# One list scheduler for a whole kernel: decayed attention and two MLPs in fp32, with quads in alternating order and five sums a quad in layer 2

## The chip, the cores and the metric

The kernel runs on one core of a Trainium2 chip. It uses the core's five instruction queues: TensorE (PE, matrix products), ScalarE (ACT), VectorE (DVE), GpSimd (POOL) and SyncE (SP, which issues the DMAs). The metric is the device time of one execution in microseconds (us). Before the change it is 615.07 us, the median of 3 runs (614.79 to 617.62).

## The reference

Three stages follow each other, all in fp32:

```python
# 1. linear attention with decay lam[h], B=2, H=8 heads, S=768, D=64, blocks of 64
intra = einsum(einsum(qb, kb) * Dmask, vb)            # Dmask[i,j] = lam**(i-j) for i >= j
out[:, :, sl] = intra + einsum(qb * lam_pow, kv_state)
kv_state = lam_block * kv_state + einsum(kb_dec, vb)
x = out.transpose(0, 2, 1, 3).reshape(1536, 512)
# 2. MLP 1: 512 -> 2048 -> 512
h = x @ w_in;  x = (h * tanh(softplus(h))) @ w_out     # Mish
# 3. MLP 2: 512 -> 2048 -> 512
h = maximum(x @ w_in, 0);  x = (h * h) @ w_out
```

## The kernel before

Every fp32 product is made of three matmuls of rounded halves: a tensor is split in a high half (a cast, on ACT) and a low half (the tensor less its high half, a subtraction), and `mm3` (L67 to L71) adds high x high, high x low and low x high in one bank of PSUM. Lines L69, L70 and L71 in the profile are these three matmuls. The 1536 tokens are four blocks t of 384.

*Weights* arrive as 64-bit patterns, in slices of 128 hidden columns (input slice io=0, output slice io=1). For each slice SP loads `raw` (L94), ACT makes `absw` (L107), DVE rebuilds the fp32 number with three integer operations (L118, L120, L122), and the result is split: cast on ACT (L138 or L199) and low half on POOL (L146 or L200).

*Attention* is 16 pairs (block t, two heads), the class `Pair`: scores, masks on DVE (L368), state updates on DVE (L363), outputs, and the split of the result into `xh` and `xl` (L398).

*Layer 1* takes the first eight hidden slices plainly, in 32 steps of one block and one slice: h (four times mm3), Mish on ACT, `gh` on ACT (L441), `gl` on POOL (L447), and four y products that accumulate in banks y0 to y3; a finished y goes to SBUF by a copy or a sum on DVE (L473). The other eight slices are taken as pairs j=0 to 3 (256 hidden columns) by two token pairs tp (blocks 2tp and 2tp+1): eight *quads*. A quad computes a 2 x 2 block product with seven products instead of eight (p1, p6, p2, p7, p4, p5, p3), which needs seven factors of the weights (sums of quarters on DVE, L234 to L240) and seven of the tokens (`first_factors`, sums at L513), and sums of the products on DVE (L657, `add`; the output tile is named u). The four results c11, c21, c22, c12 go through Mish, are split (L721, L722) and multiplied with an output slice; these y products of a quad are interleaved with the seven products of the next one as `chunks`.

*Layer 2* has 16 slices, all in 16 quads (`SecondQuad`), with relu and square (L784, L790, L791). There each of the seven products has its own turn in a ring of two banks named h, and seven DVE sums join them. Its token factors are made from layer 1's y (`right_factors`, sums at L591, splits at L579 and L583).

*What sets the order.* Attention and the first 16 steps are a table of operations with durations and due times (`plan`, L832), issued by a list scheduler (`issue`, L908): at each turn, of the operations that can start first, the one with the earliest due time. From step 16 on the order is that of the code. After each chunk of y one `job()` (L149) moves the conversion of weights on by a piece; pieces of factors lie in the list `todo`, and a few are taken behind each product; `wait_for` (L251) converts what a product asks for and isn't there yet. In layer 1 the quads run (0,0), (0,1), (1,0), (1,1), (2,0), (3,0), (2,1), (3,1) as (j, tp), every one in the same inner order, and the y banks are emptied at the end of each half of a quad's blocks.

Of the kernel before, what the change touches and what calls it, by code (L numbers as in the profile page):

```python
# [14 lines left out]
RING, RAW = 8, 5  # L15
PLAIN = 8
FIRST = (0, 4), (4, 8)
SECOND = 4
# [3 lines left out]
SLACK = 0.25  # L22
PLAN = False

# [3 lines left out]
def shares(i, n):  # L28


    if n - 1 <= i <= n + 1:
        return ((1,) * 7, (1, 1, 1, 1, 1, 0, 0), (0,) * 7)[i - n + 1], (4, 3, 3)[i - n + 1]
    return (2,) * 7, 3
# [3 lines left out]
def tile_attn_mlp_mlp(ctx, tc, qkv_in, lam, w1i, w1o, w2i, w2o, out):  # L37
    nc = tc.nc
    pe, act, dve, pool, sp = nc.tensor, nc.scalar, nc.vector, nc.gpsimd, nc.sync

# [9 lines left out]
    CPB = S // P  # L50
    blocks = [(b, c) for b in range(BATCH) for c in range(0, CPB, NC)]

    const = ctx.enter_context(tc.tile_pool(name="const", bufs=1))
    wts = ctx.enter_context(tc.tile_pool(name="wts", bufs=1))
    xp = ctx.enter_context(tc.tile_pool(name="xp", bufs=1))
    gp = ctx.enter_context(tc.tile_pool(name="gp", bufs=2))
    stg = ctx.enter_context(tc.tile_pool(name="stg", bufs=RAW))
    ac = ctx.enter_context(tc.tile_pool(name="ac", bufs=1))
    ar = ctx.enter_context(tc.tile_pool(name="ar", bufs=4))
    ps1 = ctx.enter_context(tc.tile_pool(name="ps1", bufs=1, space=PSUM))  # L60
    ps2 = ctx.enter_context(tc.tile_pool(name="ps2", bufs=2, space=PSUM))
# [997 lines left out]
```

## Time and profile before

| What | Value |
|---|---|
| median of 3 runs | 615.07 us |
| profiled execution, its own time | 619.45 us |
| its span, first to last instruction | 617.7 us |
| mean granted clock of TensorE | 0.973 |
| PE busy | 584.5 us, 95% of the span |
| DVE busy | 420.6 us, 68% |
| POOL busy | 323.9 us, 52% |
| ACT busy | 312.9 us, 51% |

The profile shows one execution. A busy share is a mean over stages with different limits, so it is read together with the table of windows, which gives busy time and the number of matmuls for each stretch of time. The granted clock is the share of full speed that PE was given: 1.00 is 2.4 GHz, and lower values in a window mean that for a part of it PE ran at the lower of its two levels. In the list of waits an entry says which engine waited, at which line, and for which other engine's instruction.

### The profile page before, as it was taken

What the parts mean: (1) busy time and instruction counts of PE and PEld (TensorE: products, weight loads), DVE (VectorE), ACT (ScalarE), POOL (GpSimd) and SP (SyncE); (2) the same over time, 40 slices, a digit from 0 to 9 for tenths busy, and PEclk for the clock granted to TensorE, in tenths of its full rate; (3) what the DMA queues carried; (4) which work ended last, traced back from release to release, by engine and by line L of the source; (5) the groups of instructions that cost most, each with busy time, mean ns of one, the idle gap of its engine ahead of it and who ended that gap; (6) DMA issues with size and microseconds to landing.
All of it is one profiled execution on the core that took longest, in us unless ns stands there. A gap on an engine that the chain in (4) does not pass through costs nothing. (4 is left out here: it accounts for less than half of the span.)

```text
span 617.7 us, 9413 instructions
## 1 busy us (share of the span) xinstructions
PE 584.5 (95%) x3448; PEld 534.7 (87%) x3448; DVE 420.6 (68%) x701; ACT 312.9 (51%) x662; POOL 323.9 (52%) x315
## 2 busy tenths in 40 slices
PE   7799999999887899999999997899999999999997
PEld 6578888999776899999999986788889989888885
DVE  5896677623998778478799693486885678464333
ACT  3464453634442544253545554667654676464441
POOL 3465343426874876272837673467562864273221
PEclk8899999999897989999999997899999999999999
DMA  8867462210420022040400120132230413000112
GB/s 313 298 211 239 119 187 71 69 35 0 137 68 1 0 70 103 0 137 1 136 1 1 34 70 34 35 102 81 91 102 1 133 38 103 1 1 0 52 52 102
DMA packets 15743, 49.89 MB, mean 81 GB/s; under 512 B 1873, under 2 KB 1873, under 8 KB 15697
## 3 DMA queue, kind: packets, MB, share of 16 engines
q1 hardware_dynamic: 15696, 49.29, 24.0%
q8 instruction: 27, 0.44, 0.3%
q14 instruction: 20, 0.16, 0.1%
HBM read 46.14 MB, written 3.15 MB: 80 GB/s over the span
## 5 line engine op out<-in xcount | busy, mean ns | idle before, releaser
L657 DVE TENSOR_TENSOR u<-h,u 128x384 f32<-128x384 f32 x120 | 65.0, 553 | 101.4 <-PE h L71 101.0
L200 POOL TENSOR_TENSOR w<-raw,w 128x256 fp32r<-128x256 f32 (+1 forms) x80 | 78.5, 997 | 17.6 <-ACT w L199 15.0
L69 PE MATMUL h<-xh,w 128*128 128x384 f32 x244 | 84.4, 346 | 0.6 <-ACT w L138 0.6
L70 PE MATMUL h<-xl,w 128*128 128x384 f32 x244 | 83.3, 341 | 1.4 <-DVE xl L398 1.4
L71 PE MATMUL h<-xh,w 128*128 128x384 f32 x244 | 83.2, 341 | 1.0 <-POOL w L146 1.0
L784 ACT ACTIVATE u<-u 128x384 f32<-128x384 f32 x64 | 33.6, 525 | 91.8 <-DVE u L657 91.4
L69 PE MATMUL y<-gh,w 128*128 128x384 f32 x192 | 68.4, 356 | 6.0 <-DVE y L473 4.3
L70 PE MATMUL y<-gl,w 128*128 128x384 f32 x192 | 66.4, 346 | 5.6 <-POOL gl L447 5.6
L447 POOL TENSOR_TENSOR gl<-u,gh 128x384 fp32r<-128x384 f32 x32 | 36.2, 1132 | 66.5 <-ACT gh L441 66.4
L71 PE MATMUL y<-gh,w 128*128 128x384 f32 x192 | 65.8, 343 | 0.1
L120 DVE SCALAR_TENSOR_TENSOR raw<-absw,raw 128x512 uint32<-128x512 uint32 x64 | 60.9, 952 | 4.6 <-ACT absw L107 1.3
L122 DVE SCALAR_TENSOR_TENSOR raw<-raw 128x512 uint32<-128x512 uint32 x64 | 56.6, 884 | 1.5
L657 DVE TENSOR_TENSOR y<-y,y 128x384 f32<-128x384 f32 (+1 forms) x88 | 49.1, 584 | 12.4 <-PE y L71 12.2
L792 POOL TENSOR_TENSOR gl<-u,gh 128x384 fp32r<-128x384 f32 x32 | 35.2, 1100 | 34.7 <-ACT u L791 19.6
L69 PEld LDWEIGHTS h<-xh,w 128*128 128x128 f32 x244 | 46.9, 192 | 5.0 <-issue 1.2
L70 PEld LDWEIGHTS h<-xl,w 128*128 128x128 f32 x244 | 46.8, 192 | 4.4 <-DVE xl L398 1.9
L71 PEld LDWEIGHTS h<-xh,w 128*128 128x128 f32 x244 | 46.5, 191 | 1.6 <-POOL w L146 1.6
L69 PEld LDWEIGHTS y<-gh,w 128*128 128x128 f32 x192 | 36.7, 191 | 10.9 <-DVE y L473 4.3
L107 ACT ACTIVATE absw<-raw 128x512 f32<-128x512 f32 x64 | 43.0, 673 | 6.0 <-DMA raw<-in_w1i_dram 3.2
L118 DVE TENSOR_SCALAR raw<-raw 128x512 uint32<-128x512 uint32 x64 | 44.7, 699 | 0.2
L199 ACT CAST w<-raw 128x256 fp32r<-128x256 f32 (+1 forms) x80 | 36.6, 493 | 15.8 <-DVE raw L122 11.5
L70 PEld LDWEIGHTS y<-gl,w 128*128 128x128 f32 x192 | 37.0, 193 | 7.5 <-POOL gl L447 7.5
(251 smaller groups left out, 1538.9 us busy)
## 6 DMA issues: line engine op xcount, KB each, us to landing
raw<-in_w1i_dram SPq DMA_DIRECT2D x16, 512.0 KB, 4.2
raw<-in_w1o_dram SPq DMA_DIRECT2D x16, 512.0 KB, 3.8
raw<-in_w2i_dram SPq DMA_DIRECT2D x16, 512.0 KB, 3.3
raw<-in_w2o_dram SPq DMA_DIRECT2D x16, 512.0 KB, 4.3
kq<-in_qkv_dram SPq DMA_DIRECT2D x16, 384.0 KB, 4.1
kv<-in_qkv_dram SPq DMA_DIRECT2D x16, 384.0 KB, 4.3
out_dram<-y SPq DMA_DIRECT2D x12, 256.0 KB, 2.0
lam_t<-in_lam_dram SPq DMA_DIRECT2D x1, 4.0 KB, 3.0
```

The source lines that it names most:

```text
L69: pe.matmul(o, lhsT=wh, rhs=xh, start=start, stop=False, **kw)
L70: pe.matmul(o, lhsT=wh, rhs=xl, start=False, stop=False, **kw)
L71: pe.matmul(o, lhsT=wl, rhs=xh, start=False, stop=stop, **kw)
L107: act.activation(a.bitcast(F32), raw[u].bitcast(F32)[:, :, 1], AF.Copy, scale=2.0 ** -112)
L118: dve.tensor_scalar(lo, lo, 29, None, op0=ALU.logical_shift_right)
L120: dve.scalar_tensor_tensor(lo, a, 3, lo, ALU.logical_shift_left, ALU.bitwise_or)
L122: dve.scalar_tensor_tensor(lo, hi, 0x80000000, lo, ALU.bitwise_and, ALU.bitwise_or)
L199: act.copy(hl[0], t)
L200: pool.tensor_tensor(hl[1], t, hl[0].bitcast(F32), ALU.subtract)
L447: pool.tensor_tensor(gl, g, gh.bitcast(F32), ALU.subtract)
L657: dve.tensor_tensor(o, x, y, ALU.add)
L792: pool.tensor_tensor(gl, u, gh.bitcast(F32), ALU.subtract)
```

## The change

`plan`, `job`, `todo`, `wait_for` and the ring allocators are gone. Every instruction of the program is now an operation `op(engine, duration, emit, reads, writes, due)`; what it must wait for follows from the names of the places that it reads and writes. One list scheduler issues all of them. Four more things change with it:

- A subtraction that makes a low half (from step 16 on) and a sum of factors may run on POOL or on DVE; the scheduler takes the engine where it can start first by its own clock. PE's operations get their due time from a running sum of durations (`slot`), and the others get theirs backwards from PE's, less a margin.
- In layer 1 the quads run (0,0), (1,0), (1,1), (0,1), (2,1), (3,1), (3,0), (2,0), and every second one takes its products in another order, with its blocks the other way round. A y bank goes on accumulating from one quad to the next where both work on the same block, and is emptied only when the block changes. In layer 2 the token pairs alternate by groups, with the same effect.
- In layer 2, p2 accumulates on the bank of p1, p4 on that of p7 and p3 on that of p5 (as layer 1 did before), so five DVE sums do instead of seven.
- SP's order of loads is the scheduler's too.

The matmuls are the same in number.

```diff
+    def op(eng, dur, emit, r=(), w=(), due=1e9, after=(), name=""):
...
+        for s in r:
+            need |= writer.get(s, set())
+        for s in w:
+            need |= writer.get(s, set()) | readers.get(s, set())
...
+    def issue():
+        for o in reversed(ops):
+            for n in o.need:
+                least = min(o.eng.values())
+                n.due = min(n.due, o.due - least - LAT - (LAND if "SP" in n.eng else 0) - (0 if "PE" in n.eng else o.early))
...
+                pick = min((x for x in c if x[0] <= r0 + SLACK), key=lambda x: (x[1].due, max(x[0], f)))
+                r = max(f, pick[0])
+                if best is None or r < best[0]:
+                    best = r, e, pick[1]
...
+    def slot(dur):
+        clock[0] += dur
+        return clock[0]
...
+    SUB384 = {"POOL": 1.1, "DVE": 0.6}
+    SUB256 = {"POOL": 0.8, "DVE": 0.5}
+    SUB512 = {"POOL": 1.4, "DVE": 0.8}
...
+    def out_slice(f):
+        if ("o", f) not in done:
+            t, R = bits(PLAIN + f, 1, [V[NI - 1]])
+            done["o", f] = split(whole_w(1, f % 5), t, R, SUB512, 0.66, name=f"o{f}")
+        return done["o", f]
...
+    SUM = {"DVE": 0.8, "POOL": 1.1}
...
+            self.order = ("p1", "p6", "p7", "p5", "p3", "p2", "p4") if turned else ("p1", "p6", "p2", "p7", "p4", "p5", "p3")
+            self.cs = ("c22", "c12", "c11", "c21") if turned else ("c11", "c21", "c22", "c12")
+            if layer:
+                z = "h0", "h1"
+                k = n % 2
+                self.bank = dict(A=z[k], B=z[1 - k], C=z[1 - k], D=z[k])
+            else:
+                self.bank = dict(A="h0", B="h1", C="X", D="Y")
...
+            op(SUB384, 0, lambda e: e.tensor_tensor(v(l), o, v(h.bitcast(F32)), ALU.subtract), O + H_, L_, name=f"gl.{self.n}")
...
+        def p4(self):
+            self.product("C", 2, "T4", True)
+            c = self.q if self.turned else self.temp("c21")
+            self.add(c, self.C, self.q)
+            self.leave("c21", c, c)
...
-        def p2(self):
-            o = self.product(bank("h")[:, :N], 1, "B21")
-            self.relu("c11", self.add(self.p, o, self.p))
...
-        def p5(self):
-            o = self.product(bank("h")[:, :N], 3, "T1")
-            self.add(self.r, o, self.r)
-            self.add(self.q, o, self.q)
-            self.relu("c22", self.r)
...
+        first = [(0, 0), (1, 0), (1, 1), (0, 1), (2, 1), (3, 1), (3, 0), (2, 0)]
...
+        for i, q in enumerate(seq):
             ys = {12: (1, 1, 1, 3, 1, 3, 2) if i else (2, 2, 2, 2, 2, 2, 0), 16: (2, 2, 2, 3, 2, 3, 2)}[len(chunks)]
-            jobs, pops = shares(i, len(order))
-            for name, y, n in zip(qd.NAMES, ys, jobs):
-                getattr(qd, name)()
-                for _ in range(n):
-                    job()
+            for name, y in zip(q.order, ys):
+                getattr(q, name)()
                 for _ in range(y):
                     chunks.pop(0)()
...
```

The change moves instructions on every queue. Three places follow, as rows of an engine's order (row number, line, operation, output and inputs, shape), before and after.

SP's queue from its first load on. Before, lam is loaded first (row 0 of both is a branch):

```order
1 L835 DMA lam_t<-in_lam_dram 128x8
2 L288 DMA kq<-in_qkv_dram 128x768
3 L293 DMA kv<-in_qkv_dram 128x768
4 L288 DMA kq<-in_qkv_dram 128x768
5 L293 DMA kv<-in_qkv_dram 128x768
6 L288 DMA kq<-in_qkv_dram 128x768
7 L94 DMA raw<-in_w1i_dram 128x1024
```

The same place of SP's queue after the change:

```order
1 L379 DMA kq_110<-in_qkv_dram 128x768
2 L381 DMA kv_114<-in_qkv_dram 128x768
3 L379 DMA kq_111<-in_qkv_dram 128x768
4 L297 DMA lam_t<-in_lam_dram 128x8
5 L381 DMA kv_115<-in_qkv_dram 128x768
6 L379 DMA kq_112<-in_qkv_dram 128x768
7 L227 DMA raw_91<-in_w1i_dram 128x1024
```

The load of lam moved from the first place to the fourth, behind two loads of kq and one of kv.

DVE's queue before, where the last pair of attention is over and the first factors and the cuts of the first weight pair begin (L118 to L122 conversion, L234 to L240 cuts of a weight pair, L513 sums of factors; their inputs z, xh, xl are factors in the making):

```order
150 L118 TENSOR_SCALAR raw<-raw 128x512
151 L120 SCALAR_TENSOR_TENSOR raw<-absw,raw 128x512
152 L122 SCALAR_TENSOR_TENSOR raw<-raw 128x512
153 L234 TENSOR_TENSOR absw<-raw 128x256
154 L513 TENSOR_TENSOR z<-xh_428,xl_429 128x384
155 L236 TENSOR_TENSOR absw<-absw,raw 128x256
156 L513 TENSOR_TENSOR z<-z 128x384
157 L238 TENSOR_TENSOR raw<-raw 128x256
158 L513 TENSOR_TENSOR z<-z 128x384
159 L240 TENSOR_TENSOR raw<-raw,absw 128x256
160 L513 TENSOR_TENSOR z<-z 128x384
161 L118 TENSOR_SCALAR raw<-raw 128x512
```

The same place after (L232 to L236 conversion, L272 cuts of a weight pair, L244 a low half of a weight):

```order
154 L232 TENSOR_SCALAR raw_93<-raw_93 128x512
155 L234 SCALAR_TENSOR_TENSOR raw_93<-absw_97,raw_93 128x512
156 L236 SCALAR_TENSOR_TENSOR raw_93<-raw_93 128x512
157 L272 TENSOR_TENSOR absw_96<-raw_93 128x256
158 L272 TENSOR_TENSOR absw_96<-absw_96,raw_92 128x256
159 L232 TENSOR_SCALAR raw_94<-raw_94 128x512
160 L234 SCALAR_TENSOR_TENSOR raw_94<-absw_97,raw_94 128x512
161 L272 TENSOR_TENSOR raw_92<-raw_92,absw_96 128x256
162 L244 TENSOR_TENSOR w_2_65<-absw_96,w_2_65 128x256
163 L236 SCALAR_TENSOR_TENSOR raw_94<-raw_94 128x512
164 L272 TENSOR_TENSOR raw_93<-raw_92,raw_93 128x256
165 L232 TENSOR_SCALAR raw_95<-raw_95 128x512
```

The sums of factors no longer stand between the cuts: the conversions of the next slices do, and one low half that POOL made before.

ACT's queue before, at the second and third quad of layer 2 (L784 relu, L790 and L791 squares, L754 the copy of p1's product; `w_0` and `w_1` with 128x512 are the output slices 10 and 11):

```order
347 L784 ACTIVATE u<-u 128x384
348 L790 ACTIVATE gh<-u 128x384
349 L791 ACTIVATE u<-u 128x384
350 L754 COPY u<-h 128x384
351 L199 CAST w_0_3767<-raw 128x512
352 L107 ACTIVATE absw<-raw 128x512
353 L784 ACTIVATE u<-u 128x384
354 L107 ACTIVATE absw<-raw 128x512
355 L790 ACTIVATE g<-u 128x384
356 L791 ACTIVATE u<-u 128x384
357 L199 CAST w_1_3822<-raw 128x512
```

The casts of the same two slices after (L616 the copy of p1's product, L243 casts, L596 relu, L606 and L607 squares; this p1 is that of layer 2's second quad, and between it and the first matmul that reads `w_0_71` stand 78 others in PE's order):

```order
343 L616 COPY u_100<-h_132 128x384
344 L243 CAST xh_79<-y_87 128x384
345 L243 CAST w_0_71<-raw_94 128x512
346 L243 CAST xh_79<-y_87 128x384 x2
347 L243 CAST w_1_72<-raw_95 128x512
348 L596 ACTIVATE u_101<-h_132 128x384
349 L606 ACTIVATE g_1632<-u_101 128x384
350 L607 ACTIVATE u_101<-u_101 128x384
```

Both casts moved up, out of the quad whose y products read the slices and into the one before it.

## Rows read from the trace of the kernel before

**Rows 1.** The page's line of totals: busy us, share of the span, instructions.
```profile
PE 584.5 (95%) x3448; PEld 534.7 (87%) x3448; DVE 420.6 (68%) x701; ACT 312.9 (51%) x662; POOL 323.9 (52%) x315
```

**Rows 2.** Windows: length; PE, PEld, DVE, ACT, POOL busy (count); clock, DMA share, GB/s.
```profile
0.00:50.00 50.00, 40.46 (x369) 32.91 (x371) 41.39 (x88) 23.31 (x52) 25.34 (x31) 0.93 0.77 272
50.00:150.00 100.00, 99.89 (x819) 91.09 (x816) 53.71 (x107) 47.31 (x100) 40.24 (x38) 1.00 0.33 102
150.00:250.00 100.00, 88.76 (x458) 83.79 (x457) 85.30 (x110) 43.52 (x95) 70.07 (x63) 0.93 0.17 59
250.00:300.00 50.00, 50.00 (x291) 49.91 (x289) 34.94 (x61) 23.28 (x51) 26.20 (x27) 1.00 0.17 53
300.00:350.00 50.00, 48.81 (x279) 48.10 (x279) 40.83 (x72) 25.68 (x54) 28.97 (x29) 1.00 0.14 43
...
360.00:400.00 40.00, 33.20 (x139) 28.31 (x139) 20.44 (x34) 20.47 (x43) 17.82 (x18) 0.87 0.17 53
400.00:550.00 150.00, 150.00 (x745) 134.93 (x744) 107.65 (x175) 95.17 (x204) 87.61 (x87) 1.00 0.20 67
```

**Rows 3.** PE's waits: line, waited for; us in total, times, longest.
```profile
PE y L70 <- POOL gl L447: 5.6, 4, 2.4
PE y L69 <- DVE y L473: 4.3, 5, 2.1
PE y L69 <- ACT w L199: 3.7, 2, 2.1
PE y L70 <- POOL w L200: 2.7, 2, 1.3
```

**Rows 4.** DVE's timeline at 127 us: start, duration, instruction, idle time before and releaser.
```profile
127.45 0.42 DVE L236 TENSOR_TENSOR absw<-absw,raw 128x256 f32<-128x256 f32 x1
148.69 1.07 DVE L513 TENSOR_TENSOR z<-z 128x384 f32<-128x384 f32 x1 [20.81 <-POOL z L513]
```

**Rows 5.** PE's timeline at the step into layer 2.
```profile
372.24 0.39 PE L69 MATMUL Y<-w,gh 128*128 128x512 f32 x1
372.47 0.39 PE L70 MATMUL Y<-w,gh 128*128 128x512 f32 x1
...
376.26 0.49 PE L69 MATMUL y<-w,g 128*128 128x512 f32 x1 [2.12 <-ACT w L199]
378.06 0.79 PE L70 MATMUL y<-w,g 128*128 128x512 f32 x1 [1.31 <-POOL w L200]
```

**Rows 6.** ACT's timeline at the same place.
```profile
375.56 0.65 ACT L199 CAST w<-raw 128x512 fp32r<-128x512 f32 x1
```

**Rows 7.** One window behind that place, columns as in rows 2.
```profile
380.00:385.00 5.00, 5.00 (x19) 4.58 (x19) 1.80 (x4) 0.31 (x1) 0.00 (x0) 0.65 0.14 56
```

**Rows 8.** DVE by line: ns least/median/most, first and last start, shapes.
```profile
L657 DVE TENSOR_TENSOR u<-h,u x120: 541/557/559, 217.9 to 603.9; 128x384 f32<-128x384 f32 x120
L657 DVE TENSOR_TENSOR y<-y,X x6: 673/676/690, 463.6 to 612.7; 128x512 f32<-128x512 f32 x6
L513 DVE TENSOR_TENSOR z<-z x16: 546/1084/1366, 148.7 to 214.1; 128x384 f32<-128x384 f32 x16
L120 DVE SCALAR_TENSOR_TENSOR raw<-absw,raw x64: 677/696/1829, 16.3 to 554.9; 128x512 uint32<-128x512 uint32 x64
```

**Rows 9.** POOL by line: the low halves of quad weights.
```profile
L200 POOL TENSOR_TENSOR w<-raw,w x80: 742/934/1468, 145.5 to 560.1; 128x256 fp32r<-128x256 f32 x56, 128x512 fp32r<-128x512 f32 x24
```

**Rows 10.** Timeline of the start: DMA issues on SP, and first uses.
```profile
0.74 0.38 SPq L835 DMA_DIRECT2D lam_t<-in_lam_dram  x1
2.11 0.43 SPq L288 DMA_DIRECT2D kq<-in_qkv_dram  x1
3.79 0.34 DVE L298 COPY lam_t<-lam_t 64x4 f32<-64x4 f32 x2 [2.66 <-DMA lam_t<-in_lam_dram]
6.41 0.80 ACT L329 ACTIVATE kv<-kv,dT 128x192 f32<-128x192 f32 x2 [4.17 <-DMA kv<-in_qkv_dram]
7.49 0.99 POOL L336 TENSOR_TENSOR qd<-kq,qs 128x384 f32<-128x384 f32 x1 [1.14 <-DMA kq<-in_qkv_dram]
```

More of the change, by code (lines that the diff above doesn't have):

```diff
@@ L39, in tile_attn_mlp_mlp @@
     pe, act, dve, pool, sp = nc.tensor, nc.scalar, nc.vector, nc.gpsimd, nc.sync
+    engine = {"PE": pe, "ACT": act, "DVE": dve, "POOL": pool, "SP": sp, "-": None}
     P = 128
@@ new lines, in pair, with Y_ @@
+        if not final:
+            op("DVE", 0.57, advance(NC - 1, S1[:, N:N + D]), [(b1, 1), *ST[2], *Q], ST[0], after=[o], due=own, name=f"A2{i}")
+    phases = [(t, 0, 4) for t in range(NB)]
+    phases += [(t, 4, 8) for t in (*range(1, NB, 2), *range(0, NB, 2))]
+    steps = [(t, f, f == f0, f == f1 - 1) for t, f0, f1 in phases for f in range(f0, f1)]
+    tmp, gs = {}, {}
+    begun = set()
+    def Y_(t, e):
+        return ysum[t][:, e * N:(e + 1) * N], [("ys", t, 3 * e + k) for k in range(3)]
@@ new lines, in evacuate @@
+    def evacuate(layer, t, e, b, due=1e9):
+        if layer:
+            o, O = ysum[t][:, e * DM:(e + 1) * DM], [("ys", t, 4 * e + k) for k in range(4)]
+            y, B, dur = bank[b], [(b, 0), (b, 1)], 0.7
+        else:
+            (o, O), y, B, dur = Y_(t, e), bank[b][:, :N], [(b, 0)], 0.56
+        if (layer, t, e) in begun:
+            op("DVE", dur, lambda en: en.tensor_tensor(o, o, y, ALU.add), B, O, due=due, name=f"YD{layer}.{t}.{e}")
+        else:
+            begun.add((layer, t, e))
+            op("ACT", dur, lambda en: en.copy(o, y), B, O, due=due, name=f"YD{layer}.{t}.{e}")
+        return o, O
@@ L651, in product @@
+            self.ny = NC if layer else KT
+            self.g, self.t, self.split = {}, {}, None
+        def product(self, b, k, name, more=False):
+            b = self.bank[b]
+            (wh, wl), W = paired(self.j)[k]
+            o = bank[b][:, :N]
             for a in range(2):
+                x, XS = factor[self.tp, name][a]
                 c = slice(a * P, (a + 1) * P)
-                mm3(o, wh[:, c], wl[:, c], *X[self.layer, self.tp, name][a], a == 0 and not more, a == 1, more)
-            return o
@@ L1005, in tile_attn_mlp_mlp @@
             assert not chunks
-            chunks = qd.chunks()
+            chunks = [lambda q=q, n=n, e=e: q.y(n, e, *flags[q.n, n, e]) for n in q.cs for e in range(q.ny)]
         for c in chunks:
             c()
+    with tc.manual_schedule():
+        pool.memset(one, 1.0)
+        act.activation(us[0][:, :1], one, AF.Mish)
+        make_identity(nc, gz[0][:, :P])
+        zero = us[1][:, :2 * P]
+        dve.memset(zero, 0.0)
+        for _ in range(WARM):
+            pe.matmul(bank["X"][:, :2 * P], lhsT=zero[:, :P], rhs=zero, start=True, stop=True)
+        for z in state + mid:
+            pool.memset(z, 0.0)
+        build()
+        issue()
```

1234 lines of the change are left out of this document (488 added, 746 removed).

## The prediction, made before the changed kernel ran

> **What bounds the kernel now.** I read the line of totals first. TensorE (PE) is busy for 584.5 of 617.7 us, VectorE (DVE) for 420.6, ScalarE (ACT) for 312.9, GpSimd (POOL) for 323.9 [rows 1]. So the time is PE's own work plus what PE loses, and the other engines count only where PE waits for them. Next the table of windows, cut at the stages [rows 2]. The reader should compare stretches by matmuls per us. From 250 to 300 PE is busy for 50.00 of 50 and does 291 matmuls, 0.172 us each: the pace of layer 1 when nothing is missing. From 400 to 550 it does 745 in 150 us, 0.2013 each: layer 2, which has longer matmuls. Against these two paces I price every other window:
> - 150 to 250 (first factors, step into the quads): 458 x 0.172 = 78.7 us of work in 100 us, so 21.3 us are lost. I call it loss A.
> - 360 to 400 (step into layer 2): 139 x 0.2013 = 28.0 us of work in 40 us, 12.0 lost: loss B.
> - 300 to 350: 279 x 0.172 = 47.9 in 50, 2.1 lost: loss C.
> - 0 to 50: PE is idle for 9.5 us. 50 to 150: 99.89 busy of 100, nothing lost; 400 to 600: nothing.
> A and B hold more than direct waits. The list of PE's waits [rows 3] has 4.3 us for a y sum of DVE, 5.6 for a low half of g from POOL, 3.7 and 2.7 for halves of a weight. The rest is clock: behind the gaps at 376 us the window 380 to 385 is granted 0.65, and 19 matmuls take 5 us there [rows 7], where 25 fit at layer 2's pace; the means of the windows are 0.93 (A) and 0.87 (B) against 1.00 [rows 2].
>
> **Loss A: what ends last.** DVE's timeline [rows 4] shows DVE idle for 20.81 us, from 127.9 to 148.69, because a factor sum (L513) waits for POOL at the head of its queue. Then everything that was due comes at once: DVE is busy for 85.3 us of 150 to 250, against 53.71 of the 100 us before [rows 2]. PE's y products and low halves come late there. The change puts all of this under one scheduler: DVE's rows behind the last pair are conversions and cuts of weights with nothing of the factors at their head (the piece of DVE's order). So the 20.81 us are filled with work that before fell behind 148.69, and the rush is gone. What remains: DVE's old work of 128 to 250, some 85 us, now has 122 us, 0.70; factor sums leave it and low halves come (below), so I take about 0.75. Two planned stretches bracket that: 50 to 150, with DVE at 0.54, lost nothing; 0 to 50, with DVE at 0.83, lost 9.5 of 50 us. I keep 3 of 21.3 and take **-18.3** (bounds: -21.3 if it is like 50 to 150; if it is like 0 to 50, 19% of 100 us stays, and the gain is 2).
>
> **Loss B.** At 376.26 a y product starts that has waited 2.12 us for ACT's cast of an output slice of w2 (L199), and at 378.06 it has waited 1.31 more for POOL's low half [rows 5]. The cast itself began at 375.56 and ended 0.05 before the product [rows 6]: it is issued only when the y product asks for it, behind the copy of p. After the change the cast of the same slice stands in ACT's order at the p copy of the quad *before* (piece of ACT's order), and 78 matmuls lie between that quad's p1 and the product that reads it: 78 x 0.2013 = 15.7 us for a cast of 0.65 [rows 6] and a low half of at most 1.47 [rows 9]. So both waits go, and with them the low clock that followed [rows 7]. I keep 3 of 12.0 for the factors of layer 2, which still start when the last y sum of layer 1 is done: **-9.0** (bounds -12 and 0).
> **Loss C**: single late sums among quads, half kept: **-1.0**. The 9.5 us of 0 to 50 stay: that part was list-scheduled before and its operations are the same.
>
> **Start.** SP issued lam first (0.74 us), and DVE's first use came at 3.79, 3.05 later [rows 10]. Now lam is fourth; the fourth issue stood at 2.11, so the same delay gives 5.16, +1.4. If instead it lands behind the three loads ahead of it (the second and third of them were first used at 6.41 and 7.49 [rows 10], now issued one place of some 0.4 sooner), lam comes at about 7.1, +3.3. DVE's start is not all that PE waits for there, so 0 is the lower end. I take **+1.5**, near the first (0 to +3.3). Beside this, the Trainium skill ("DMA: Bandwidth & Descriptors", "Two DMAs through the same engine are not ordered") says descriptors of one queue start in order; the two uses 1.1 us apart agree, and by it the sum would carry +3.3.
>
> **Layer 2's shared banks.** p2, p4 and p3 now accumulate on the bank of p1, p7 and p5 after a sum has read it, so PE waits if that sum is late. Between p7 and p4, and between p5 and p3, stand three y products: 9 matmuls at 0.23 [rows 5] = 2.07 us, against 0.557 for DVE's sum [rows 8] once it is at the head of the queue. 32 such places (16 quads x 2). I take **+1.0** (0 to +35; the upper end is worked out below).
>
> **DVE and POOL work.** The counts are of the two orders. DVE's u sums go from 152 to 120: 32 x 0.557 = 17.8 us; 384-wide y sums of layer 1 from 80 to 60, 512-wide of layer 2 from 36 to 18: 20 x 0.557 + 18 x 0.676 = 23.3; factor sums on DVE from 40 to 20: 20 x 1.084 = 21.7 [rows 8]. New on DVE are 89 low halves that POOL did (13 of L449, 44 of L610, 32 of weights): alone 0.55 each, 49 us; with the L513 row's median 1.084, 96 us. DVE then has 407 to 454 us, POOL 239 instructions instead of 313. Both lie under PE's work, so I count **0** for all of them; layer 2 before, with DVE at 107.65 of 150, already lost nothing.
> What a moved low half costs is the open size. L657's sums, with one input in PSUM, never leave 541 to 559 ns; L513, two inputs in SBUF, goes from 546 to 1366, and L120 up to 1829 [rows 8]. The Trainium skill ("SBUF — State Buffer", "Who interferes with whom") says that DVE's second port pair is shared with GpSimd as an exclusive lock, so one of two such operations stands still until the other is done. The two rows agree with that. By the rule each moved low half could cost 0.55 plus a POOL operation's 0.934 [rows 9], 89 x 1.48 = 132 us: DVE at 490, still below PE, but queued in front of urgent sums. It speaks against the change and for the slower rival.
>
> **The sum.** -18.3 - 9.0 - 1.0 + 1.5 + 1.0 = -25.8. The profiled execution took 619.45 (span 617.7 and 1.75 around it): 593.65. It stood 4.38 above the median of the runs, 615.07, so I predict **589**.
>
> **Rivals.**
> 1. *The fixed order gives half back.* The scheduler plans with constants (0.6 for a low half on DVE, 0.85 for L120), but rows show up to 1.37 and 1.83 [rows 8]. A queue can't be changed on the chip, so an operation that is late holds what stands behind it, and new gaps bring low clock. For it: A was such a case, made by a planned piece meeting hand-written ones. Against it: 50 to 150 was planned with the same kind of constants and lost nothing. Half of 25.8: about 602 (598 to 610).
> 2. *The waits aren't the order's doing.* If A and B come from buffers (plain weights must be read before quarters can overwrite them, y of all four blocks must be summed before layer 2's factors), issuing earlier changes little. If only 9 us of A come back: -9 - 1 + 1.5 + 1 = -7.5, 607.6; with half of that, 612. Against it: the casts before were asked for late, in the code (wait_for), and DVE's queue held conversions behind the waiting L513 sum.
> 3. *Slower: layer 2's sums come late.* Its place is the 32 turns p7 to p4 and p5 to p3. The sum can stand behind one stretched operation of 1.83 (L120's maximum): 1.83 + 0.56 - 2.07 = 0.3 late; behind two of 1.3 (L513's, near its maximum): 2.6 + 0.56 - 2.07 = 1.1 late, and 32 x 1.1 = 35 us, without the clock. From 25.8 / 32 = 0.8 us a place the whole gain is gone; at 1.1 the time is 589 + 35 - 1 = 623. For it: 44 low halves of g and 32 of weights now share DVE's queue with these sums. Against it: five sums a quad instead of seven and half the y sums, and rows where DVE at 72% was never late.
>
> **How the numbers follow.** Forecast 0.68 (580 to 598), rival 1 0.15, rival 2 0.07, rival 3 0.10. The range 579 to 607 holds the forecast and most of rival 1, about 0.8. A measurement of this kernel can tell a change of about 0.5%: 612.0 to 618.1 counts as the same. Faster: 0.68 + 0.15 + 0.02 of rival 2 = 0.85; same: 0.05 of rival 2; slower: rival 3, 0.10.
>
> **What would show it.** Right: no idle stretch of DVE above some 5 us between the last pair and the first quad; windows of the former 150 to 250 at 0.172 to 0.18 us a matmul; no wait of y for ACT's or POOL's half of a weight in PE's list; clock 1.00 in nearly all windows after 50 us and a mean of about 0.99; first lam copy between 5 and 7 us; layer 2 at 0.2013 a matmul. Wrong: PE waiting for DVE's u sums again and again in layer 2 (rival 3), a new group of waits for low halves (rival 1), or the same stall at the step into layer 2 with the casts early (rival 2).

## The result: faster, by some six tenths of what was forecast

The changed kernel takes 601.02 us (median of 4 runs, 599.04 to 601.85); the kernel before, run beside it, 616.35. The ratio is 0.9741 with a 95% interval of 0.9691 to 0.9791. The forecast was faster, 589 us, range 579 to 607. The time lies in the range, but 12 us above the forecast: 2.6% less where the forecast had 4.2. The profiled execution took 601.85 us, its span is 599.9 (before 619.45 and 617.7) and the mean granted clock 0.989.

The line of totals after the change answers to [rows 1]:

```profile
PE 577.1 (96%) x3448; PEld 528.8 (88%) x3448; DVE 428.6 (71%) x705; ACT 319.5 (53%) x662; POOL 254.0 (42%) x241
```

DVE has 8 us more than before and POOL 70 less, as the counts said; PE's matmuls are the same. The windows of the changed kernel, columns as in [rows 2]; the sixth is cut at 340, to hold the whole step into layer 2:

```profile
0.00:50.00 50.00, 38.15 (x335) 31.04 (x336) 37.68 (x80) 22.87 (x50) 24.06 (x32) 0.90 0.74 253
50.00:150.00 100.00, 98.89 (x813) 87.89 (x812) 75.33 (x132) 51.44 (x111) 53.52 (x48) 1.00 0.40 122
150.00:250.00 100.00, 99.96 (x576) 99.46 (x575) 73.63 (x115) 45.14 (x96) 44.76 (x40) 1.00 0.12 43
250.00:300.00 50.00, 49.89 (x288) 49.57 (x287) 40.52 (x68) 24.63 (x51) 19.46 (x20) 1.00 0.24 85
300.00:340.00 40.00, 39.17 (x222) 37.96 (x221) 34.33 (x54) 23.96 (x52) 26.15 (x24) 1.00 0.11 40
340.00:400.00 60.00, 56.53 (x270) 49.65 (x269) 54.94 (x74) 44.90 (x94) 42.03 (x36) 0.97 0.20 71
400.00:550.00 150.00, 148.50 (x734) 132.93 (x733) 92.21 (x152) 88.22 (x178) 40.95 (x40) 1.00 0.15 50
```

Read it in three places. From 150 to 250 PE now does 576 matmuls in 100 us where it did 458, at the dense pace. The first 50 us do 335 matmuls instead of 369. And at the step into layer 2 PE waits, with DVE busy for 54.94 of 60 us; layer 2 itself, which lost nothing before, does 734 instead of 745 in its 150 us.

PE's list of waits, to set beside [rows 3]:

```profile
PE h L189 <- DVE u L590: 5.1, 5, 1.9
PE X L340 <- DMA kq<-in_qkv_dram: 3.2, 1, 3.2
PE h L190 <- DVE xl L402: 1.8, 1, 1.8
PE y L334 <- ACT kv L344: 1.6, 2, 0.8
...
PE y L190 <- POOL gl L449: 0.8, 2, 0.6
```

Of the four waits of before three are gone, and the one for a low half of g fell from 5.6 to 0.8 us. In their place stand five for DVE's sums of products (L590 is the former L657) and one for a load at the start.

To compare stages of kernels whose order differs I use one number: PE's lost time, the time at which a matmul starts less the dense time of all matmuls that started before it. Dense times are taken near the median spacings of starts in the two traces (0.174 us for 384 columns, 0.232 for 512): 0.1735 and 0.233, with 0.07 for a short matmul of attention and 0.427 for those of the warm-up. The columns are the lost time that each stretch adds, in us; E1 to E12 are the experiments below.

| kernel | 0-60 | 60-150 | 150-280 | 280-340 | 340-400 | 400-580 | sum |
|---|---|---|---|---|---|---|---|
| before | 14.6 | 1.1 | 20.8 | 1.8 | 12.3 | 1.1 | 51.6 |
| after | 19.1 | 3.1 | 0.4 | 2.2 | 6.6 | 3.0 | 34.4 |
| E1 lam first | 16.5 | 2.9 | -0.1 | 2.5 | 6.3 | 3.0 | 31.1 |
| E2 low halves on POOL | 17.4 | 2.9 | 2.8 | 3.2 | 6.5 | 3.1 | 36.1 |
| E3 seven sums | 19.9 | 3.0 | 0.4 | 1.7 | 2.6 | 1.0 | 28.6 |
| E4 old quads | 18.4 | 3.3 | 3.8 | 1.9 | 3.7 | 1.1 | 32.1 |
| E5 lam first, seven sums | 17.9 | 2.7 | -0.1 | 1.7 | 2.6 | 1.0 | 25.8 |
| E6 E5 with old quads | 16.3 | 2.9 | 4.1 | 1.9 | 3.1 | 1.0 | 29.3 |
| E7 before, five sums | 11.1 | 2.2 | 20.0 | 1.8 | 8.1 | 1.0 | 44.2 |
| E8 before, more jobs | 13.1 | 1.1 | 19.5 | 1.8 | 8.4 | 1.0 | 44.9 |
| E9 E1, longer durations | 13.5 | 1.5 | 2.6 | 0.4 | 1.0 | 3.4 | 22.5 |
| E10 E5, longer durations | 15.7 | 1.4 | 2.6 | 0.0 | 1.6 | 0.9 | 22.2 |
| E11 E1, conversion 0.95 | 19.3 | 3.2 | 0.5 | 1.3 | 3.8 | 1.0 | 29.1 |
| E12 E5, conversion 0.95 | 17.3 | 3.3 | 0.5 | 1.3 | 2.3 | 1.0 | 25.6 |

Before less after is 17.2 us, the spans differ by 17.8. Each row is one execution, and the first column carries noise: before, E7 and E8 have the same code there and differ by 3.5 us; they were granted 0.94, 1.00 and 0.94 of the clock in those 60 us, the changed kernel 0.91. E9's execution (590.17 us) is 5 us faster than the median of its runs, and the only one granted the full clock throughout.

**Where the u sums are late.** DVE's timeline of the changed kernel at the longest of those waits, and PE's matmul that waited:

```profile
349.45 1.25 DVE L532 TENSOR_TENSOR y<-y,y 128x384 f32<-128x384 f32 x1
350.63 1.50 DVE L244 TENSOR_TENSOR w<-raw,w 128x512 fp32r<-128x512 f32 x1
352.06 1.35 DVE L244 TENSOR_TENSOR xl<-y,xh 128x384 fp32r<-128x384 f32 x1
353.33 0.55 DVE L590 TENSOR_TENSOR u<-h,u 128x384 f32<-128x384 f32 x1
```

```profile
351.67 0.39 PE L191 MATMUL y<-w,w 128*128 128x512 f32 x1
353.93 0.45 PE L189 MATMUL h<-dT,w 128*128 128x384 f32 x1 [1.88 <-DVE u L590]
```

This is p4 on the bank of p7: its three y products are done, and the sum that must read the bank first is queued behind a factor sum and two low halves, of which the weight's (128x512) was POOL's before the change. In the scheduler's plan the three take 0.8, 0.8 and 0.6 us; on the chip 1.25, 1.50 and 1.35, while POOL works beside them. From the start of the first to the start of the sum 3.88 us pass where the plan has 2.2, and PE waits 1.88. The sum itself takes 0.55, as everywhere. The window around this wait:

```profile
350.00:360.00 10.00, 8.12 (x31) 6.82 (x31) 10.00 (x11) 5.26 (x11) 9.43 (x8) 0.83 0.16 52
```

DVE is busy all the time and POOL nearly so. Behind the wait PE is granted the lower clock for a while (0.83 in the mean), and does 31 matmuls where layer 2's pace gives about 50. So the loss at the step is waits (3.4 us from 340 to 400) and clock together.

**The start.** The first lines of SP, DVE and PE in the changed kernel, for [rows 10]:

```profile
2.10 0.43 SPq L297 DMA_DIRECT2D lam_t<-in_lam_dram  x1
8.88 0.34 DVE L301 COPY lam_t<-lam_t 64x4 f32<-64x4 f32 x2 [7.75 <-DMA lam_t<-in_lam_dram]
10.82 0.58 PE L340 MATMUL X<-kq 64*128 64x128 f32 x1 [3.16 <-DMA kq<-in_qkv_dram]
```

lam is used 6.78 us after its issue, not 3.05.

### The profile page after: what moved, and what is told of

The parts are those of the page before. It is cut to its first block, busy times and chain, and to the rows that moved or that the text cites. A ratio compares the mean times of both kernels' runs of the same rounds, so it can differ in the third digit from the quotient of the medians.

```text
span 599.9 us, 9221 instructions
## 1 busy us (share of the span) xinstructions
PE 577.1 (96%) x3448; PEld 528.8 (88%) x3448; DVE 428.6 (71%) x705; ACT 319.5 (53%) x662; POOL 254.0 (42%) x241
## 4 chain that ended last, share of the span: by engine, by line
PE 72%; DVE 14%; POOL 5%; issue 4%; DMA 3%; ACT 1%; SPq 0%; POOLq 0%; DVEq 0%; ACTq 0%
PE y L189 10%; PE y L190 10%; PE y L191 9%; PE h L189 9%; PE h L191 9%; PE h L190 8%; PE X L190 2%; PE Y L189 2%; PE Y L191 2%; PE X L191 2%; PE Y L190 2%; PE X L189 2%; POOL w L244 2%; DVE u L590 2%; DVE raw L236 2%
## 5 line engine op out<-in xcount | busy, mean ns | idle before, releaser
L244 POOL TENSOR_TENSOR w<-raw,w 128x256 fp32r<-128x256 f32 (+1 forms) x72 | 82.7, 1155 | 79.8 <-ACT w L243 69.3
L590 DVE TENSOR_TENSOR u<-h,u 128x384 f32<-128x384 f32 x88 | 48.8, 554 | 55.8 <-PE h L191 55.2
L596 ACT ACTIVATE u<-u 128x384 f32<-128x384 f32 x72 | 37.9, 527 | 72.0 <-DVE u L590 71.3
L189 PE MATMUL y<-gh,w 128*128 128x384 f32 x192 | 66.8, 348 | 0.2
L243 ACT CAST w<-raw 128x256 fp32r<-128x256 f32 (+1 forms) x96 | 48.7, 523 | 29.3 <-DVE raw L236 20.4
L191 PE MATMUL y<-gh,w 128*128 128x384 f32 x192 | 64.3, 335 | 0.0
L234 DVE SCALAR_TENSOR_TENSOR raw<-absw,raw 128x512 uint32<-128x512 uint32 x64 | 56.9, 889 | 6.5 <-ACT absw L230 2.4
L610 POOL TENSOR_TENSOR g<-u,g 128x384 fp32r<-128x384 f32 x20 | 21.2, 1058 | 94.5 <-PE h L191 80.4
L236 DVE SCALAR_TENSOR_TENSOR raw<-raw 128x512 uint32<-128x512 uint32 x64 | 55.8, 872 | 1.0
L230 ACT ACTIVATE absw<-raw 128x512 f32<-128x512 f32 x64 | 43.0, 676 | 17.3 <-DVE raw L234 7.1
L425 DVE TENSOR_TENSOR y<-y,y 128x384 f32<-128x384 f32 (+1 forms) x72 | 39.6, 571 | 9.5 <-PE y L191 9.0
L232 DVE TENSOR_SCALAR raw<-raw 128x512 uint32<-128x512 uint32 x64 | 41.3, 646 | 2.4 <-DMA raw<-in_w2o_dram 2.2
L190 PEld LDWEIGHTS y<-gl,w 128*128 128x128 f32 x192 | 36.1, 188 | 1.7 <-POOL gl L449 1.5
L449 POOL TENSOR_TENSOR gl<-u,gh 128x384 fp32r<-128x384 f32 x19 | 21.0, 1104 | 36.3 <-ACT gh L447 35.5
```

Source lines behind the costliest of these rows:

```text
L189: pe.matmul(o, lhsT=wh, rhs=h, start=start, stop=False, **kw)
L190: pe.matmul(o, lhsT=wh, rhs=l, start=False, stop=False, **kw)
L191: pe.matmul(o, lhsT=wl, rhs=h, start=False, stop=stop, **kw)
L230: op("ACT", 0.68, lambda e: e.activation(absw[a].bitcast(F32), word.bitcast(F32)[:, :, 1], AF.Copy, scale=2.0 ** -112), R, A, after=after, ...
L232: op("DVE", 0.55, lambda e: e.tensor_scalar(lo, lo, 29, None, op0=ALU.logical_shift_right), [], R, after=last.get("bits", ()), name=f"CB{F ...
L234: op("DVE", 0.85, lambda e: e.scalar_tensor_tensor(lo, absw[a], 3, lo, ALU.logical_shift_left, ALU.bitwise_or), A, R, name=f"CC{F}.{io}")
```

## The experiments

My theories after the result: (1) lam's fourth place costs the start; (2) the low halves moved to DVE fill it at the step into layer 2; (3) alternation and five sums are off the path; and, once E2 and E3 had spoken, (4) the scheduler's clock for DVE runs ahead of the chip, and the shared banks are where that costs; (5) what is left of the start is DVE's order there. Each run was timed beside the kernel before; ratios are to that kernel, with 95% intervals.

**E1: lam first.**

```diff
-        o = op("SP", 1.05, lambda e: e.dma_start(out=kq[n4], in_=qkv_in[t, p, :, 0:2]), [], KQ, after=last.get("kq", ()), name=f"kq{i}")
+        o = op("SP", 1.05, lambda e: e.dma_start(out=kq[n4], in_=qkv_in[t, p, :, 0:2]), [], KQ, after=last.get("kq") or writer["lam"], name=f"kq{i}")
```

> The changed kernel with one edit: the load of lam is SP's first again, all else is the scheduler's. Theory 1 (lam's fourth place costs the start): lam's first copy on DVE moves from 8.88 us back to about 3.8, the last attention matmul comes some 4 us earlier than 121.2, the time falls by 3 to 5 us, to 596 to 598 where the changed kernel has 601. Rival (the start is slower because of the new order of the attention's own operations and of the weight loads): below 1.5 us, 599.5 to 601.

Measured: 599.33 us, ratio 0.9688 (0.9647 to 0.9729). lam's first copy is back at 3.75 us, the last matmul of attention starts at 119.8 instead of 121.2 (4 us were expected), and lost time to 60 us falls from 19.1 to 16.5. Between theory and rival; the intervals of E1 and of the changed kernel overlap, so the 2.6 us are the trace's word alone, and they are within the noise of that column. Some of the start's loss is not lam's.

**E2: low halves on POOL.**

```diff
-    SUB384 = {"POOL": 1.1, "DVE": 0.6}
-    SUB256 = {"POOL": 0.8, "DVE": 0.5}
-    SUB512 = {"POOL": 1.4, "DVE": 0.8}
+    SUB384 = {"POOL": 1.1}
+    SUB256 = {"POOL": 0.8}
+    SUB512 = {"POOL": 1.4}
```

(and the same for the low half of g in the plain steps).

> The changed kernel with all low halves (subtractions of splits) on POOL, as before the change; the sums of factors still choose. DVE has 105 operations less. Theory 2 (the low halves moved to DVE, stretched to 1.0 to 1.5 us beside POOL, fill DVE at the step into layer 2 and make its u sums late): the waits of PE for DVE's u (5.1 us in all) go, DVE's busy share between 340 and 380 us falls from 0.98 to under 0.85, the time falls by 3 to 6 us, to 595 to 598. Rival (POOL alone can't make the low halves in time at the steps; the choice of engine is what removed the stalls): new waits of PE for POOL at 120 to 160 and at 340 to 380 us, the time rises by 5 to 12 us, to 606 to 613.

Measured: 606.19, ratio 0.9806 (0.9774 to 0.9837): 0.7% behind the changed kernel, with intervals that just overlap, and in no case the gain expected. Theory 2 falls, and the rival's place is wrong too. PE's list of waits of E2:

```profile
PE h L189 <- DVE u L590: 6.8, 5, 1.8
PE X L340 <- DMA kq<-in_qkv_dram: 3.6, 1, 3.6
PE X L189 <- DVE u L590: 1.7, 1, 1.7
PE y L190 <- POOL gl L449: 1.5, 3, 0.6
```

PE still waits for DVE's sums, longer than before the edit. The window at the step tells why:

```profile
340.00:400.00 60.00, 55.00 (x272) 48.24 (x271) 53.34 (x65) 44.27 (x94) 57.03 (x49) 1.00 0.21 71
```

DVE has 65 operations where it had 74, but is busy for 53.34 us instead of 54.94, and POOL is busy for 57.03 of 60. The same operation, the last of the weight conversion on DVE, least/median/most ns over the whole kernel, first in the changed kernel and then in E2:

```profile
L236 DVE SCALAR_TENSOR_TENSOR raw<-raw x64: 676/694/1697, 23.4 to 519.0; 128x512 uint32<-128x512 uint32 x64
L236 DVE SCALAR_TENSOR_TENSOR raw<-raw x64: 682/1124/1509, 22.8 to 520.7; 128x512 uint32<-128x512 uint32 x64
```

Its median goes from 694 to 1124 ns. The lock between the two engines that the Trainium skill describes ("SBUF — State Buffer", "Who interferes with whom") agrees with these rows: work taken from DVE and given to POOL comes back as longer operations of DVE.

**E3: seven sums in layer 2, undoing the shared banks.**

```diff
             b = self.bank[b]
+            if self.layer:
+                b = ("h0", "h1")[next_of("turn", 2)]
...
         def p4(self):
+            if self.layer:
+                c = self.add(self.temp("c21"), self.product("C", 2, "T4"), self.t["r"])
+                return self.leave("c21", c, c)
...
             self.add(r, self.D, r)
+            if self.layer:
+                self.add(self.q, self.D, self.q)
```

(p2, p6 and p3 likewise.)

> The changed kernel with layer 2's products back on a bank of their own each and seven DVE sums a quad (32 sums of 0.557 us more on DVE, 17.8 us; no wait for a sum between two products of one bank). Theory 3 (the spared sums are off PE's path, since PE loses only 2 us between 400 and 600 us): within 1.5 us of the changed kernel, 600 to 602.5. Rival (with low halves on DVE the room is needed): the DVE share of 400 to 550 rises from 0.61 to above 0.75, u sums come late, 4 to 10 us slower, 605 to 611. A third: the two waits of the shared banks go and it is 2 us faster, 599.

Measured: 595.21, ratio 0.9627 (0.9599 to 0.9655), clearly faster than the changed kernel. All three expectations fail in size; the third had the sign. The windows of E3:

```profile
340.00:400.00 60.00, 58.53 (x292) 52.05 (x291) 57.18 (x87) 46.86 (x98) 40.47 (x37) 1.00 0.26 85
400.00:550.00 150.00, 150.00 (x743) 134.74 (x742) 100.15 (x169) 89.88 (x182) 44.78 (x43) 1.00 0.13 44
```

DVE does more there (57.18 of 60), and PE 22 matmuls more. A product that goes to the other bank needs the sum of two products ago, so a late sum is no wait yet: PE's waits for DVE's sums on h fall from 5.1 to 1.4 us.

```profile
PE h L189 <- DVE u L592: 1.4, 2, 0.9
```

Lost time after 340 falls from 9.6 to 3.6: in the order of the changed kernel the shared banks cost 6.0 us.

**E4: the old order of quads, none turned.**

```diff
-        first = [(0, 0), (1, 0), (1, 1), (0, 1), (2, 1), (3, 1), (3, 0), (2, 0)]
+        first = [(0, 0), (0, 1), (1, 0), (1, 1), (2, 0), (3, 0), (2, 1), (3, 1)]
...
-            qs_.append(Quad(n, 0, j, tp, n % 2 == 1))
+            qs_.append(Quad(n, 0, j, tp, False))
```

(and the token pairs of layer 2 in one fixed order.)

> The changed kernel with the old order of quads, none turned, so y banks are emptied 36 times a block pair more often: 20 sums of 384 and 12 of 512 columns more on DVE and 6 copies less spared on ACT. Theory 3 (off the path where PE is dense): within 2 us of the changed kernel in layer 2 and the dense part of layer 1, and at most 2 more at the step into layer 2, where DVE is full: 600 to 604. Rival (the alternation is what made the step into layer 2 shorter, because the token pair that layer 2 starts with is finished earlier): the loss at the step grows from 6 to 9 or more us, 604 to 609.

Measured: 599.69, ratio 0.9705 (0.9675 to 0.9735): not told apart from the changed kernel. As theory 3 has it in sum, but not in place: 3.4 us more are lost in 150 to 280 and 4.8 less after 340.

**E5: lam first and seven sums.** The edits of E1 and E3 together.

> The changed kernel with both edits that helped alone: lam loaded first, and layer 2 with seven sums on banks of their own. If the two costs are independent (start 2.7 us of PE's lost time, shared banks 5.5), the sum gives 601 - 2.7 - 5.5 = 593, ratio to the kernel before 0.958 to 0.961. Rival (the scheduler orders everything anew and what one edit gave is lost again elsewhere): 594.5 to 597.

Measured: 591.29, ratio 0.957 (0.9535 to 0.9605). The two add up. It beats the kernel before and the changed kernel, whose interval begins at 0.9691.

**E6: E5 with the old quads,** so that the scheduler alone is left of the change.

> The same with the old order of quads, none turned: so of the change the one list scheduler with its choice of engine alone is left (lam first, seven sums, old quads). Theory (the scheduler is the whole gain; alternation and five sums give nothing on the path): within 2 us of the kernel with lam first and seven sums, 591 to 595. Rival (alternation's spared 32 sums on DVE make the room for seven sums): DVE full at the step into layer 2, PE waits there for u sums again, 4 to 8 us more, 597 to 601.

Measured: 597.09, ratio 0.967 (0.9637 to 0.9703), 1% behind E5. The rival has the size but not the place: the step into layer 2 loses 3.1 us against 2.6, and the stretch from 150 to 280 loses 4.1 against none. PE's waits there in E6, first a low half of g, then a y sum:

```profile
PE y L190 <- DVE gl L449: 2.3, 1, 2.3
...
PE y L189 <- DVE y L425: 0.9, 2, 0.5
```

So alternation is worth about 6 us when nothing else is in its way, and 4.2 us of lost time lie where the first factors are made. From 150 to 250 DVE is busy for 82.68 us in E6 and for 73.31 in E5. E4 and E6 also show what the shared banks cost with the old quads (E6 has lam first besides): 4.8 and 4.1 us are lost after 340, so 0.7 us instead of 6.0. The price of a shared bank depends on the order around it.

**E7: the kernel before with five sums.**

```diff
         def p4(self):
-            o = self.product(bank("h")[:, :N], 2, "T4")
-            self.relu("c21", self.add(temp(), o, self.r))
+            self.product(self.C, 2, "T4", more=True)
+            self.relu("c21", self.add(temp(), self.C, self.q))
```

(p2 and p3 likewise, two banks that change roles from quad to quad.)

> The kernel before with one part of the change alone: five sums a quad in layer 2, p2, p4 and p3 on the banks of p1, p7 and p5. Theory (shared banks make PE wait only where DVE's queue is full of stretched operations, which the kernel before has at the step into layer 2 alone, all low halves being on POOL): 0 to 3 us slower than before, 616 to 620, with PE's waits for DVE's u near 360 to 400 us. Rival 1 (shared banks cost in every quad): 10 us or more slower. Rival 2 (spared DVE work helps): 1 to 4 us faster.

Measured: 613.49, ratio 0.9919 (0.9886 to 0.9951): faster, rival 2 (5 us, where it had 1 to 4). The same edit that costs 6 us in the scheduled kernel gains here; of the 7.4 us that the table has between the two, 3.5 lie in the noisy first column and 4.2 in 340 to 400 (12.3 to 8.1). The waits of layer 2 are still those for the halves of a slice, and on the shared banks (h) PE waits for a sum of DVE once, 0.5 us:

```profile
PE y L70 <- POOL w L200: 2.4, 2, 1.5
PE y L69 <- ACT w L199: 2.0, 2, 1.1
...
PE h L69 <- DVE u L657: 0.5, 1, 0.5
```

That one wait stands in the kernel before as well, at the same product, so the shared banks added none. The hand-written order issues each sum right behind its product, with nothing new in front of it, and DVE is not full there: from 340 to 400 it is busy for 37.99 us, 54.94 in the changed kernel. So a shared bank does not cost by itself; whether DVE's load or the order ahead of the sum makes it cost, E7 does not tell.

**E8: the kernel before with conversions going on at the step.**

```diff
-        return ((1,) * 7, (1, 1, 1, 1, 1, 0, 0), (0,) * 7)[i - n + 1], (4, 3, 3)[i - n + 1]
+        return (2,) * 7, (4, 3, 3)[i - n + 1]
```

> The kernel before with the conversion of weights going on at full rate across the step into layer 2 (two jobs behind each product also for the three quads there), so that the casts of output slices 10 and 11 stand about one quad earlier in ACT's order; nothing else moves by design. Theory (loss B is the late cast): PE's waits for ACT's and POOL's halves of the slice (3.7 and 2.7 us) go with their low clock, 4 to 9 us faster, 608 to 613. Rival (DVE's load at the step sets it; the conversions only crowd out the factors): PE waits for DVE's u or the factors instead, between 3 faster and 5 slower.

Measured: 613.53, ratio 0.994 (0.9914 to 0.9966): faster, with the theory's sign and just under its size (0.6% are 3.7 us, and 4 to 9 were expected). PE's waits for the halves of a slice are gone from the list, and this line has grown from 0.5 us:

```profile
PE h L69 <- DVE u L657: 3.9, 2, 2.1
```

Lost time at the step falls by 3.9 us (12.3 to 8.4). What comes in place of the casts is DVE's sums, and the edit brings that about itself. The window at the step in the kernel before and in E8:

```profile
340.00:400.00 60.00, 53.20 (x252) 47.95 (x251) 35.35 (x59) 33.86 (x73) 31.11 (x32) 0.91 0.14 45
340.00:400.00 60.00, 54.88 (x271) 48.87 (x270) 53.95 (x79) 40.82 (x88) 42.05 (x37) 0.97 0.21 71
```

DVE had 59 operations and 35.35 us there before; in E8 it has 79 and 53.95, nearly the 54.94 of the changed kernel. What was added is conversion: of its three integer operations 8 run there before, 24 in E8 and 25 in the changed kernel. So the theory holds for the casts, and the rival for what takes their place.

**E9: longer durations in the plan,** with lam first and the shared banks kept.

```diff
-    SUB384 = {"POOL": 1.1, "DVE": 0.6}
-    SUB256 = {"POOL": 0.8, "DVE": 0.5}
-    SUB512 = {"POOL": 1.4, "DVE": 0.8}
+    SUB384 = {"POOL": 1.2, "DVE": 1.1}
+    SUB256 = {"POOL": 0.95, "DVE": 0.7}
+    SUB512 = {"POOL": 1.5, "DVE": 1.2}
...
-    SUM = {"DVE": 0.8, "POOL": 1.1}
+    SUM = {"DVE": 1.2, "POOL": 1.2}
```

(and the low half of g in the plain steps, on DVE from 0.7 to 1.0).

> The changed kernel with lam first (five sums, shared banks, turned quads kept), and with the scheduler's durations of low halves and factor sums on DVE raised to what the trace shows where POOL works too: 384 columns 0.6 to 1.1, 512 0.8 to 1.2, 256 0.5 to 0.7, sums 0.8 to 1.2 us (POOL's 1.1 to 1.2). Theory 4 (u sums come late for the shared banks because the scheduler's clock for DVE runs ahead of the chip at the step into layer 2): PE's waits for DVE's u there and at 462 us (5.1 us in all) fall under 2.5 and the lost time after 340 us from 8.9 to 5 or less; the time 3 to 4 us below that of lam first alone (598 to 599), 594 to 596. Rival (DVE is simply full there, whatever the order; only banks of their own help): within 1.5 us of lam first alone.

Measured: 595.19, ratio 0.9645 (0.9612 to 0.9677), where E1 has 0.9688 (0.9647 to 0.9729): the intervals just overlap. The granted clock differs from run to run, so compare at like clock: E1's two runs at 1.00 take 595.34 and 595.98 us and its four at 0.988 to 0.994 take 598.42 to 600.96; E9's one at 1.00 takes 590.17 and its five at 0.985 to 0.994 take 594.73 to 595.34. The window of E9 at the step and PE's waits for sums in the whole kernel:

```profile
340.00:400.00 60.00, 59.59 (x295) 53.15 (x294) 54.60 (x75) 44.72 (x93) 38.23 (x33) 1.00 0.21 71
PE h L189 <- DVE u L590: 2.4, 4, 1.5
PE X L189 <- DVE u L590: 1.9, 1, 1.9
```

With DVE as full as in the changed kernel (54.60 of 60, 75 operations) PE does 295 matmuls instead of 270; lost time there falls from 6.3 to 1.0. So DVE's load does not set the loss; the order does. Nothing changed but numbers in the plan, and with them which operation stands ahead of which, and for a dozen operations which engine makes them (DVE has 691, in E1 703). One wait for a sum, of 1.5 us at 454, stays, and 400 to 580 still loses 3.4; a new one on bank X, of 1.9 us at 205, is most of the 2.6 lost in 150 to 280.

That the better durations did it, and not just another order, E9 does not show alone. E4, with the old durations, loses 4.8 us less after 340 than the changed kernel, about as much as E9 loses less than E1 (4.9).

**E10: the same with seven sums. E11: E1 with the integer operations' duration at 0.95 instead of 0.85. E12: E5 with that duration.** The edit of E11 and E12:

```diff
-        op("DVE", 0.85, lambda e: e.scalar_tensor_tensor(lo, absw[a], 3, lo, ALU.logical_shift_left, ALU.bitwise_or),
+        op("DVE", 0.95, lambda e: e.scalar_tensor_tensor(lo, absw[a], 3, lo, ALU.logical_shift_left, ALU.bitwise_or),
...
-        o = op("DVE", 0.85, lambda e: e.scalar_tensor_tensor(lo, hi, 0x80000000, lo, ALU.bitwise_and, ALU.bitwise_or),
+        o = op("DVE", 0.95, lambda e: e.scalar_tensor_tensor(lo, hi, 0x80000000, lo, ALU.bitwise_and, ALU.bitwise_or),
```

> The same raised durations with lam first and seven sums on banks of their own. Theory 4: little is left to win at the step there (two waits, 1.5 us), so within 1.5 us of the kernel with lam first and seven sums, 590 to 593. Rival (more low halves go to POOL, and it is late at 120 to 180 us as with all of them on POOL): 2 to 5 us slower, 594 to 597.

> The changed kernel with lam first and with the scheduler's duration of the two longer integer operations of the weight conversion back at 0.95 us, as the kernel before had it (the change has 0.85). Theory 5 (what stays lost at the start with lam first, 16.8 us of PE's time to 60 us against 11.0 to 14.6 before, is DVE's order there: conversions put in front of the low halves of attention): the lost time to 60 us falls to 14 or less and the time by 2 to 4 us against lam first alone, to 595 to 597. Rival (the start is lost by the order of PE and SP): within 1 us, 598 to 599.

> Lam first, seven sums on banks of their own, and the integer operations' duration back at 0.95 us: the combination of the edits that helped. Theory 4: what the longer duration gave beside the shared banks was later u sums at the step into layer 2 (9.2 us lost after 340 us fell to 4.7); with banks of their own only 3.5 us are lost there, so at most 1 us is left to win: ratio to the kernel before 0.954 to 0.958, 590 to 592 us. Rival (the longer duration helps in other places too): 0.950 to 0.953.

Measured: E10 592.2, ratio 0.9591 (0.956 to 0.9623), as theory 4 has it: with banks of their own better durations save nothing in sum (2.8 us less lost after 280 than in E5, 2.7 more in 150 to 280). E11 595.03, ratio 0.9652 (0.962 to 0.9684), is in the range that theory 5 gave but for another reason: the start loses 19.3 us, no less, and the gain lies at the step (6.3 to 3.8) and behind it (3.0 to 1.0). Theory 5 has no support; since E11's first 60 us were granted 0.89 of the clock and E1's 0.94, the column could hide a gain of some 2 us. E12 593.26, ratio 0.9596 (0.9565 to 0.9627): no better than E5. E5, E10 and E12 are equal within their intervals, at about 0.958.

## Why the prediction was right in sign and too high in gain

- **Loss A, -18.3: right.** 150 to 280 loses 0.4 us instead of 20.8, and 60 to 150, where the work went, 3.1 instead of 1.1: -18.4. DVE's longest idle stretch there is 3.6 us, 20.81 before, and it is busy for 75.33 and 73.63 of 100 us, as taken (0.75). The mechanism is read in the trace; no run undoes it alone. E6, with the scheduler alone, loses 4.1 us from 150 to 280, so alternation, which the working did not name, gave about 4 of the gain there.
- **Loss B, -9.0, and C, -1.0: half.** The mechanism was right for the casts: no wait for half of a slice is left at the step. But 340 to 400 still loses 6.6 and 280 to 340 2.2, -5.3 together. The working named the factors as the remainder and gave them 3 us; it did not ask what moving the conversions earlier would put on DVE there: 35.35 of 60 us busy before, 54.94 after. E8 shows the same trade in the kernel before: earlier casts, a full DVE (53.95), and 3.9 us of waits for its sums.
- **Layer 2's shared banks, +1.0: the mis-sized term.** It measured +6.0 (E3; 0.7 with the old quads), 4.0 at the step, counted under B above, and 2.0 after 400. The step that failed is the comparison of 2.07 us with "0.557 for DVE's sum once it is at the head of the queue": the question was what stands at the head. Rival 3 described just this, and its price a place was of the right kind (0.3 us behind one stretched operation, 1.1 behind two; the trace shows 1.9 behind three), but it charged 32 places; there were 5 waits in all, at the step and at 466 us, where DVE is full. Its argument against, DVE at 72% and never late, was a mean, and so hid these few places.
- **Start, +1.5: too small.** 14.6 to 19.1 in the profiles, with 3.5 us of noise in that column. lam's first use came at 8.88, beyond the upper bound of 7.1, and +5.1 against before. A start in order behind the loads ahead of it, as the Trainium skill has it ("DMA: Bandwidth & Descriptors", "Two DMAs through the same engine are not ordered"), gave +3.3, nearer than my +1.4. Even that bound failed: the third load landed 5.0 us after its issue, at 6.6, and lam only at 8.9; why so small a load came 2.2 us behind it is not shown. E1 gives back 2.6 us; the rest of the start's loss is open.
- **DVE's and POOL's work, 0: right as a sum.** DVE has 428.6 us, inside 407 to 454. A low half of g on DVE takes a median of 0.558, not 1.084:

```profile
L610 DVE TENSOR_TENSOR gl<-u,gh x27: 545/558/1369, 247.9 to 588.8; 128x384 fp32r<-128x384 f32 x27
L532 DVE TENSOR_TENSOR y<-y,y x6: 1069/1308/1369, 310.5 to 356.4; 128x384 f32<-128x384 f32 x6
```

DVE gets these low halves mostly where POOL is idle: 39 of the 44 of L610 run with no operation of POOL beside them, while factor sums at the step meet a busy POOL. By E2 the choice of engine is worth about 0.7% (0.9806 against 0.9741), with intervals that just overlap.

In sum: -18.4 - 5.3 + 4.5 + 1.9 = -17.3 where -25.8 was forecast. For the part after 340 what happened is close to rival 1 (about 602, a chance of 0.15): a fixed order in which an operation that runs late holds a sum that PE needs. The order is shown as the cause by E9, with the same load on DVE and the same banks. That the plan's short durations made that order is shown at the longest wait (3.88 us against 2.2), and beyond it argued, since E4's order does as well with the old ones. The start's part (4.5 against 1.5) is not rival 1's, so that the time fell on rival 1's 602 is partly luck.

What stays open: why the start loses 16 to 19 us in most scheduled kernels with lam first or not, against 11 to 15 before, while E9 and E10 lose 13.5 and 15.7 there. A part of it is clock. E1 and E9 do 235 and 237 matmuls in their first 30 us; from 30 to 40 E1 is granted 0.68 and does 50, E9 is granted 1.00 and does 83. What lets the clock fall in one execution and not in another is not shown.

## What to carry to other kernels

When a list scheduler sets every queue, its durations are part of the kernel: give it what an operation takes beside its busy neighbour (here that gave 4 us, though another order did as well), and look at the place where an engine is full, not at its mean share; an edit that moves work earlier may be what fills it. Two products that share a bank turn a late sum into a wait of the bounding engine at once; a second bank hides it, and an edit that spares work on an engine off the path can therefore cost time in one order (6.0 us) and next to nothing in another (0.7). Try the parts of a change apart: here one part gave the gain, one helped only beside another, and one took back a quarter.

## What the runs showed of the hardware

- Four KB of lam, issued fourth at 2.10 us, were used 6.78 us after the issue; issued first at 0.74, 3.05 after [rows 10].
- Taking work from DVE to POOL made the operations left on DVE longer: the 64 of L236 went from a median of 694 to 1124 ns (E2).
- Low halves of 384 columns on DVE, both inputs in SBUF: 49 ran with no operation of POOL beside them and took at most 560 ns; of the 30 that met one, 24 took longer, up to 1.37 us (changed kernel).
- A DVE sum with one input in PSUM took 543 to 558 ns in every place of the changed kernel, between neighbours with both inputs in SBUF that took up to 1.50 us beside POOL.
